# Moving the crossbar transposes, the mask and the casts of a block-sparse attention kernel

## The chip, the cores and the metric

The kernel runs on one core of a Trainium2 chip. The metric is the device time of one execution in microseconds. Before the change it was 378.04 us (median of 2 runs, 377.01 to 379.08). The profile is of one execution; its span, from the first to the last instruction, is about 2 us shorter than the time. A run counts as slow when it is over 1.5% above the fastest of the same kernel; ratios use fast runs alone, while medians are over all runs.

The engines are named as in the profile: PE (TensorE, matmuls), PEld (its weight loads), DVE (VectorE), ACT (ScalarE), POOL (GpSimd) and SP (SyncE, which issues most of the loads). The granted clock is the share of PE's full clock that the profile records. A crossbar transpose is a transpose done by a DMA.

## The reference

```python
# q, k, v: 4 batches x 8 heads x 768 x 64, float32
scores = q @ k.T / sqrt(64)
scores = where(mask, scores, -1e9)   # mask of 24 x 24 blocks of 32: window, edges, 3 random ones a row
attn = softmax(scores); x = attn @ v         # heads laid side by side: 4 x 768 x 512
h = x.T @ U @ V                              # rank 32
u = x + h.T
out = u + relu(u @ w_ch1) @ w_ch2            # 512 -> 2048 -> 512
```

## The kernel before

Heads are worked on in pairs, 16 pairs in all, four to a batch. A pair has six key tiles g and two query halves c, so twelve steps. At each step PE makes the scores of both heads (`psc`), ACT takes the exponential (`est`), and PE multiplies it with v (`pav`). After a pair comes its tail: DVE normalizes (`xs`), POOL casts (`xh`), PE multiplies with U (`pa`) and V (`ph`), DVE adds (`xf`), POOL casts (`uh`), and a crossbar transpose on the SP queue makes `uT`, the input of the MLP. In batches 1 to 3 the MLP of the batch before is cut into small pieces that fill PE between the score steps (`run_fill`). The last MLP runs alone at the end.

Each q and k is loaded, cast to fp16 (`qst`, `kst`) and transposed (`qT`, `kT`).

```python
def load_qk(i, cast):                      # load and cast of pair i, together
    for src, nm in ((q, "q"), (k, "k")):
        ld = ldpool.tile(...)
        nc.sync.dma_start(out=ld, in_=src[...])
        st = stpool.tile(...)
        cast[nm].tensor_copy(out=st..., in_=ld)      # POOL

def turn_dma(sts):                         # crossbar transposes on the SP queue
    for st, nm in zip(sts, "qk"):
        nc.sync.dma_start_transpose(out=tt, in_=st...)

def scores(i, g, c, est, on_pe):
    for h in range(2):                     # two 64-row matmuls
        mm(psc[:, h, 0:HS], kT[rows[h], kc], qT[rows[h], qc], True, not on_pe)
    if on_pe:                              # batch 0: the mask is added by PE
        for h in range(2):
            mm(psc[:, h, 0:HS], kb[rows[h], kc], oh[rows[h], qc], False, True)
    nc.scalar.activation(out=est[:, c], in_=psc[...], func=AF.Exp, scale=0.125)

for i in range(HP):                        # batch 0
    for g in range(T):
        for c in range(2):
            scores(i, g, c, est, True)
            ...                            # value matmuls run two steps behind
        if g == 0: sts[i + 2] = load_qk(i + 2, cast)
        if g == 1: load_v(i + 2)
        if g == 2:
            if i == 1: load_w1()           # 2 MB each, issued from POOL
            if i == 3: load_w2()
        if g == 3:
            qkT[i + 1] = turn_pe(...) if i < 1 else turn_dma(...)

for i in range(HP, NPAIR):                 # batches 1 to 3: the mask is a DVE multiply (mask_mul)
    for g in range(T):
        for c in range(2): scores(i, g, c, est, False)
        ...                                # mask_mul, finish_pair (tail of the pair before), run_fill
        if g == 0: sts[i + 2] = load_qk(i + 2, cast)
        if g == 1: load_v(i + 2)
        if g == 3: qkT[i + 1] = turn_dma(...)
```

The softmax here doesn't subtract the row's maximum and nothing guards it: scores larger than these inputs give would overflow.

## Time and profile before

| | before |
|---|---|
| time | 378.04 us |
| span of the profiled run | 375.2 us |
| PE, ACT, DVE busy | 82%, 47%, 46% |
| mean granted clock of PE | 0.904 |
| pair 4 begins at | 93.7 us |
| last exp begins at | 315.7 us |

"Pair n begins" is the start of every twelfth exponential in the trace, here and below; the "tail" of the tables is what comes after the start of the last one.

Two rows of the page's second part, in which the span is cut into 40 slices of 9.4 us and each digit is a share in tenths:

```profile
PE   1985078850799999795699997987899999999995
PEclk9999559585589999999599999998899999999999
```

PE is idle in the fifth and the tenth slice, and its clock is at half there and just after. The view of waits gives the cause (who waited for whom: us in total, times, longest):

```profile
POOL qst L140 <- DMA qld<-in_q_dram: 33.7, 8, 6.1
...
PE psc L104 <- DMA kT<-kst: 28.4, 3, 14.5
...
PE pa L104 <- POOL xh L331: 15.1, 15, 3.6
...
PE pt L104 <- DMA uT<-uh: 7.8, 3, 4.0
```

POOL stands 33.7 us in q casts whose load has not landed, and PE waits 15.1 us for the `xh` casts that POOL also does. The longest wait of PE, 14.5 us, is for a transposed k. The timeline around it (start, duration, engine, line, operation, in brackets the idle time before it and who ended it):

```profile
30.40 2.15 POOL L262 DMA_DIRECT2D w1t<-in_moe_w_ch_dram  x4
...
31.85 1.78 SPq L181 DMA_TRANSPOSE qT<-qst  x1
...
33.68 10.20 SPq L181 DMA_TRANSPOSE kT<-kst  x1
43.92 0.58 SPq L132 DMA_DIRECT2D qld<-in_q_dram  x1
...
48.17 0.50 PE L104 MATMUL psc<-qT,kT 64*128 64x384 f16 x2 [14.53 <-DMA kT<-kst]
```

The 2 MB of w1 go out at 30.40 us from POOL, the transposes of pair 2 right behind from SP. The second of these keeps the SP queue for 10.20 us and lands, as PE's wait shows, 14.5 us after its issue; a k transpose with no weight load beside it, issued at 61.64 us, landed after 2.6 us. The Trainium skill, "Trainium Kernel Development and Optimization", Key Constraints, says that DMAs of the SP, ACT and POOL queues run on the same 16 DMA engines and interleave. This trace agrees: the transposes were issued from another queue than the weights and were still delayed by them. The same happens with w2 at 75.3 us.

Windows of the same stretch. The columns are the window, its length, then busy us (and instructions) of PE, PEld, DVE, ACT and POOL, the granted clock, the share of the DMA engines, and GB/s:

```profile
30.00:40.00 10.00, 3.64 (x51) 1.72 (x50) 0.00 (x0) 4.24 (x6) 2.55 (x5) 0.91 0.87 147
40.00:50.00 10.00, 1.83 (x14) 0.62 (x14) 0.49 (x2) 0.81 (x1) 0.00 (x0) 0.50 1.17 221
50.00:60.00 10.00, 8.65 (x92) 4.29 (x91) 3.90 (x10) 5.46 (x7) 4.34 (x7) 0.74 0.06 22
```

PE does little for 15 us, and when it starts again it runs at 0.50, then 0.74.

### The profile page before, as it was taken

The numbers are of one execution on the slowest core, as the hardware profiler recorded it, in microseconds if no ns is written. First come the engines' busy times: TensorE is split into PE (matmuls) and PEld (weight loads), VectorE is DVE, ScalarE is ACT, GpSimd is POOL, SyncE is SP. The second block draws the span as 40 slices with busy tenths as digits, with TensorE's granted clock in tenths as the row PEclk, the third lists the DMA queues.
The fourth block names the chain that finished last, engine by engine and source line by source line (L and its number), as shares of the span: only waits on it lengthen the run. The fifth ranks groups of instructions, "written<-read, shape, count | busy, mean of one in ns | idle before, by whom it ended". The sixth has DMA issues, their size and how long they took to land. (4 is left out here: it accounts for less than half of the span.)

```text
span 375.2 us, 6642 instructions
## 1 busy us (share of the span) xinstructions
PE 307.9 (82%) x2759; PEld 155.8 (42%) x2759; DVE 173.8 (46%) x298; ACT 175.8 (47%) x258; POOL 89.9 (24%) x129
## 2 busy tenths in 40 slices
PE   1985078850799999795699997987899999999995
PEld 0342034330345553433255644442456454556442
DVE  3130023330456766455467764563477755444221
ACT  1676037440567765444367754443477663033100
POOL 3734031440232131413131414141121121200000
PEclk9999559585589999999599999998899999999999
DMA  7816944299390044438340906264802011210011
GB/s 241 237 69 104 170 140 89 103 125 163 113 247 2 19 137 112 154 100 217 103 90 2 189 21 204 69 202 54 189 2 65 3 49 58 73 56 2 28 68 72
DMA packets 55657, 38.82 MB, mean 103 GB/s; under 512 B 37548, under 2 KB 52012, under 8 KB 55628
## 3 DMA queue, kind: packets, MB, share of 16 engines
q1 hardware_dynamic: 51760, 33.93, 34.6%
q0 software_dynamic: 3472, 4.24, 7.1%
q8 instruction: 21, 0.34, 0.4%
q10 hardware_dynamic: 396, 0.24, 0.2%
q14 instruction: 8, 0.07, 0.1%
HBM read 27.70 MB, written 6.29 MB: 91 GB/s over the span
## 5 line engine op out<-in xcount | busy, mean ns | idle before, releaser
L301 ACT ACTIVATE est<-psc 128x768 f16<-128x768 f32 x192 | 145.3, 809 | 108.9 <-PE psc L104 108.7
L104 PE MATMUL pt<-uT,w1t 128*128 128x384 f16 x512 | 96.0, 341 | 7.8 <-DMA uT<-uh 7.8
L104 PE MATMUL pch<-w2t,tT 128*128 128x512 f16 x384 | 92.1, 388 | 0.0
L104 PE MATMUL psc<-qT,kT 64*128 64x384 f16 x384 | 58.3, 355 | 29.9 <-DMA kT<-kst 28.4
L308 DVE TENSOR_TENSOR est<-est,m 128x1536 f16<-128x1536 f16 x72 | 71.8, 997 | 0.7 <-ACT est L301 0.6
L104 PEld LDWEIGHTS <-w1t 128*128 128x128 f16 x512 | 49.8, 101 | 44.5 <-issue 18.1
L402 ACT ACTIVATE tT<-pt 128x384 f16<-128x384 f32 x64 | 31.5, 492 | 55.7 <-PE pt L104 55.2
L404 DVE TENSOR_SCALAR tT<-pt 128x384 f16<-128x384 f32 x64 | 35.6, 557 | 46.6 <-PE pt L104 45.7
L104 PEld LDWEIGHTS <-tT 128*128 128x128 f16 x384 | 36.2, 99 | 40.1 <-issue 4.9
L104 PEld LDWEIGHTS <-est 128*128 128x128 f16 x1152 | 41.5, 99 | 26.4 <-issue 25.8
L104 PE MATMUL pav<-vt,est 128*128 128x65 f16 x1152 | 50.5, 197 | 0.0
L373 POOL CAST uh<-xf 128x384 f16<-128x384 f32 x32 | 20.9, 656 | 98.7 <-DVE xf L369 57.9
L104 PEld LDWEIGHTS <-kT 64*128 64x128 f16 x384 | 14.1, 95 | 63.1 <-issue 30.6
L331 POOL CAST xh<-xs 128x384 f16<-128x384 f32 x32 | 20.4, 636 | 71.4 <-DVE xs L324 67.9
L420 DVE TENSOR_TENSOR of<-xf,pch 128x512 f32<-128x512 f32 x24 | 16.5, 687 | 40.6 <-PE pch L104 40.6
L369 DVE TENSOR_TENSOR xf<-xs,ph 128x384 f32<-128x384 f32 x32 | 17.5, 551 | 18.3 <-PE ph L104 18.2
L321 DVE RECIPROCAL rcp<-pav 128x6 f32<-128x6 f32 x32 | 6.2, 195 | 40.8 <-PE pav L104 40.6
L140 POOL CAST qst<-qld 128x768 f16<-128x768 f32 x15 | 12.7, 846 | 51.8 <-DMA qld<-in_q_dram 33.7
L104 PE MATMUL pa<-xh,Ut 128*128 128x128 f16 x96 | 11.0, 239 | 15.4 <-POOL xh L331 15.1
L104 PE MATMUL psc<-oh,kb 64*128 64x384 f16 x96 | 19.7, 385 | 0.5 <-ACT kb L242 0.5
L324 DVE TENSOR_TENSOR xs<-pav,rcp 128x384 f32<-128x384 f32 x32 | 17.8, 557 | 2.1
L359 DVE CAST a<-pa 128x128 f16<-128x128 f32 x16 | 4.6, 288 | 26.4 <-PE pa L104 26.4
(38 smaller groups left out, 94.1 us busy)
## 6 DMA issues: line engine op xcount, KB each, us to landing
qld<-in_q_dram SPq DMA_DIRECT2D x16, 384.0 KB, 3.4
kld<-in_k_dram SPq DMA_DIRECT2D x16, 384.0 KB, 4.3
vld<-in_v_dram SPq DMA_DIRECT2D x16, 384.0 KB, 5.2
out_dram<-of SPq DMA_DIRECT2D x24, 256.0 KB, 2.0
w1t<-in_moe_w_ch_dram POOLq DMA_DIRECT2D x4, 512.0 KB, 11.8
w2t<-in_moe_w_ch_dram POOLq DMA_DIRECT2D x4, 512.0 KB, 11.8
uT<-uh SPq DMA_TRANSPOSE x16, 2.5
qT<-qst SPq DMA_TRANSPOSE x14, 2.5
```

The source lines that it names most:

```text
L104: nc.tensor.matmul(out, lhsT, rhs, start=start, stop=stop, skip_group_check=loose)
L140: keep(cast[nm].tensor_copy(out=st.rearrange("p t h d -> p h t d"), in_=ld))
L301: nc.scalar.activation(out=est[:, c], in_=psc[:, :, 0:HS], func=AF.Exp, scale=0.125)
L308: nc.vector.tensor_tensor(out=est, in0=est, in1=m01[:, g].rearrange("p (c n) -> p c n", c=2)[:, :, None, :] .broadcast_to([P, 2, 2, HS]), ...
L321: keep(nc.vector.reciprocal(out=rcp, in_=pav[:, :, :, D]))
L324: nc.vector.tensor_tensor(out=x3.rearrange("p j (h d) -> p j h d", h=2), in0=pav[:, :, :, 0:D], in1=rcp[:, :, :, None].broadcast_to([P, 3, ...
L331: keep(nc.gpsimd.tensor_copy(out=xh[:, 3 * c : 3 * c + 3, :], in_=x3))
L369: nc.vector.tensor_tensor(out=u3, in0=xs[:, 3 * c : 3 * c + 3, :], in1=ph, op=ALU.add)
L373: keep(nc.gpsimd.tensor_copy(out=uh[:, 3 * c : 3 * c + 3, :], in_=u3))
L402: keep(nc.scalar.activation(out=dst, in_=pt, func=AF.Relu))
L404: keep(nc.vector.tensor_scalar_max(out=dst, in0=pt, scalar1=0.0))
L420: keep(nc.vector.tensor_add(out=of, in0=xfs[b][:, sc, :], in1=pchs[sc]))
```

## The change

Its intent: keep crossbar transposes away from the weight loads by transposing batch 0 on PE; take the mask matmuls off PE; issue the loads of batch 0 further ahead; and cast later than the load is issued, so that POOL does not stand waiting. Cut to its core:

```diff
 # pair 0: the 64 rows of q and of k get 64 mask rows beside them, one 128-row matmul a head
+            if i == 0:
+                mm(psc[:, h, 0:HS], ka[h][:, kc], qa[h][:, qc], True, True)
 # pairs 1 to 3: DVE multiplies instead of mask matmuls on PE
-                scores(i, g, c, est, True)
+                scores(i, g, c, est)
+                if i > 0:
+                    mask_mul(g, est, c)
-    VLAG = 2
+    VLAG = 3                                     # value matmuls three steps behind
-                later.extend(pair_tail(i, xs, xh))
+                later.extend([(0, lambda: None)] * 2 + pair_tail(i, xs, xh))
 # pairs 1 to 4: transposed by PE, one tensor at a time
-                qkT[i + 1] = turn_pe(sts.pop(i + 1)) if i < 1 else turn_dma(sts.pop(i + 1))
+                if i < 3 and u in (6, 8): ... turn_pe(i + 1, nm); nc.vector.tensor_copy(...)
+                if i == 3 and u in (8, 10): ... the same
 # batches 1 to 3
+            if g == 0:
+                turn_dma(i + 1, "q"); turn_dma(i + 1, "k"); issue(i + 2)
+            if g == 2:
+                cast(i + 2, "q")
+            if g == 4:
+                cast(i + 2, "k"); cast(i + 2, "v")
-            if i == HP and g == 2:
+            if i == HP and g == 4:
                 fill.extend(mlp_steps(0))
-            if g == 0 and i + 2 < NPAIR:
-                sts[i + 2] = load_qk(i + 2, cast)
-            if g == 1 and i + 2 < NPAIR:
-                load_v(i + 2)
-            if g == 3 and i + 1 < NPAIR:
-                qkT[i + 1] = turn_dma(sts.pop(i + 1))
# (cut: places of the loads in batch 0, the building of the 0/1 mask moved into pair 0, the last value matmuls of batch 0 spread over pair 4, buffer counts)
```

More of the change, by code (lines that the diff above doesn't have):

```diff
@@ L66 @@
     pos = (cols % P) * T + cols // P
-    oh_np = np.zeros((2, D, S), dtype=np.float16)
-    oh_np[:, :NB] = (pos[None, :] // BLK == ii[:, None])[None]
-    oh_np = oh_np.reshape(P, S)
+    oh_np = np.zeros((D, S), dtype=np.float16)
+    oh_np[:NB] = pos[None, :] // BLK == ii[:, None]
     eye16_np = np.eye(P, dtype=np.float16)
@@ L80 @@
     stpool = ctx.enter_context(tc.tile_pool(name="stpool", bufs=2))
-    qkpool = ctx.enter_context(tc.tile_pool(name="qkpool", bufs=3))
+    qkpool = ctx.enter_context(tc.tile_pool(name="qkpool", bufs=2))
     epool = ctx.enter_context(tc.tile_pool(name="epool", bufs=10))
@@ L109 @@
     id16 = consts.tile([P, P], FP16)
-    oh = consts.tile([P, S], FP16)
-    kb = consts.tile([P, S], FP16)
+    qa = [consts.tile([P, S], FP16, name=f"qa{h}") for h in range(2)]
+    ka = [consts.tile([P, S], FP16, name=f"ka{h}") for h in range(2)]
     m01 = consts.tile([P, T, S], FP16)
@@ L123, with issue @@
     rows = [slice(0, D), slice(D, P)]
-    def load_qk(i, cast):
+    mrows = [slice(D, P), slice(0, D)]
+    lds, sts, qkT = {}, {}, {}
+    NPAIR = B * HP
+    def issue(i, names="qkv"):
+        if i >= NPAIR:
+            return
         b, hp = divmod(i, HP)
-        sts = []
-        for src, nm in ((q, "q"), (k, "k")):
+        for nm in names:
             ld = ldpool.tile([P, 2, T, D], FP32, tag="ld" + nm, name=nm + "ld")
+            src = {"q": q, "k": k, "v": v}[nm]
             keep(
@@ L138, in load_qk, with cast @@
             )
-            st = stpool.tile([P, T, 2, D], FP16, tag="st" + nm, name=nm + "st")
-            keep(cast[nm].tensor_copy(out=st.rearrange("p t h d -> p h t d"), in_=ld))
-            sts.append(st)
-        return sts
-    def load_v(i):
-        b, hp = divmod(i, HP)
-        ld = ldpool.tile([P, 2, T, D], FP32, tag="ldv", name="vld")
+            lds[i, nm] = ld
+    def cast(i, nm, eng=None):
+        if i >= NPAIR:
+            return
+        b, hp = divmod(i, HP)
+        ld = lds.pop((i, nm))
+        if nm == "v":
+            keep(
+                nc.gpsimd.tensor_copy(
+                    out=vts[b % 2][:, 2 * hp : 2 * hp + 2, :, 0:D], in_=ld
+                )
+            )
+            return
+        st = stpool.tile([P, T, 2, D], FP16, tag="st" + nm, name=nm + "st")
@@ L147, in load_v, with turn_pe @@
         keep(
-            nc.sync.dma_start(
-                out=ld,
-                in_=v[b, 2 * hp : 2 * hp + 2].rearrange("h (p t) d -> p h t d", t=T),
-            )
-        )
+            (eng or nc.gpsimd).tensor_copy(
+                out=st.rearrange("p t h d -> p h t d"), in_=ld
+            )
+        )
+        sts[i, nm] = st
+    def turn_pe(i, nm):
+        st = sts.pop((i, nm))
+        pt = pst_tile([P, T, P], FP16, "pturn")
+        for t in range(T):
+            keep(
+                nc.tensor.transpose(
+                    out=pt[:, t, :],
+                    in_=st[:, t].rearrange("p h d -> p (h d)"),
+                    identity=id16,
+                )
+            )
+        return pt
@@ L153, in load_v, with new_turn, turn_dma @@
+    def new_turn(i, nm):
+        qkT[i, nm] = qkpool.tile([P, T, P], FP16, tag=nm + "T", name=nm + "T")
+        return qkT[i, nm]
+    def turn_dma(i, nm):
+        if i >= NPAIR:
+            return
+        st = sts.pop((i, nm))
         keep(
-            nc.gpsimd.tensor_copy(
-                out=vts[b % 2][:, 2 * hp : 2 * hp + 2, :, 0:D], in_=ld
-            )
-        )
-    def turn_pe(sts):
-        ts = []
-        for st, nm in zip(sts, "qk"):
-            pt = pst_tile([P, T, P], FP16, "pturn")
-            for t in range(T):
-                keep(
-                    nc.tensor.transpose(
-                        out=pt[:, t, :],
-                        in_=st[:, t].rearrange("p h d -> p (h d)"),
-                        identity=id16,
-                    )
-                )
-            tt = qkpool.tile([P, T, P], FP16, tag=nm + "T", name=nm + "T")
-            keep(nc.vector.tensor_copy(out=tt, in_=pt))
-            ts.append(tt)
-        return ts
@@ L176, in turn_dma @@
-    def turn_dma(sts):
-        ts = []
-        for st, nm in zip(sts, "qk"):
-            tt = qkpool.tile([P, T, P], FP16, tag=nm + "T", name=nm + "T")
-            keep(
-                nc.sync.dma_start_transpose(
-                    out=tt, in_=st.rearrange("p t h d -> p (t h d)")
-                )
-            )
-            ts.append(tt)
-        return ts
+            nc.sync.dma_start_transpose(
+                out=new_turn(i, nm), in_=st.rearrange("p t h d -> p (t h d)")
+            )
+        )
@@ L192 @@
     nc.scalar.dma_start(out=small[0:NB, :], in_=small_dr.ap())
+    nc.scalar.dma_start(out=id16, in_=eye16_dr.ap())
     nc.scalar.dma_start(out=dup[0:NB], in_=dup_dr.ap())
-    nc.scalar.dma_start(out=id16, in_=eye16_dr.ap())
-    nc.scalar.dma_start(out=oh, in_=oh_dr.ap())
-    sts = {}
-    qkT = {}
-    sts[0] = load_qk(0, {"q": nc.vector, "k": nc.gpsimd})
+    for h in (1, 0):
+        nc.scalar.dma_start(out=qa[h][mrows[h], :], in_=oh_dr.ap())
+    issue(0)
+    issue(1)
     for vt in vts:
@@ L218 @@
         prev = a01[0:NB]
+        if r == 0:
+            cast(0, "q", nc.vector)
     keep(
@@ L224 @@
     )
+    cast(0, "k")
+    pq = turn_pe(0, "q")
     pb = pst_tile([P, 2 * D], FP32, "pb")
@@ L231 @@
     )
-    qkT[0] = turn_pe(sts.pop(0))
+    pk = turn_pe(0, "k")
     pm = pscp.tile([P, 2, 512], FP32, tag="psc", name="pm")
@@ L237 @@
             bias[0:NB].rearrange("k a z -> k (a z)"),
-            oh[0:NB, c * HS : (c + 1) * HS],
+            qa[1][0:NB, c * HS : (c + 1) * HS],
             True, True,
         )
-    keep(
-        nc.scalar.copy(
-            out=kb.rearrange("z (c n) -> z c n", c=2), in_=pm[:, :, 0:HS]
-        )
-    )
-    def load_mix():
-        nc.gpsimd.dma_start(
-            out=Ut[:, :, 0:R], in_=moe_U.rearrange("(p t) r -> p t r", t=T)
-        )
-        vld = ldpool.tile([P, S], FP32, tag="ldv", name="mvld")
-        keep(nc.sync.dma_start(out=vld[0:R, :], in_=moe_V))
+    flat = "p t n -> p (t n)"
+    keep(nc.vector.tensor_copy(out=qa[0][rows[0], :], in_=pq[rows[0]].rearrange(flat)))
+    keep(nc.scalar.copy(out=qa[1][rows[1], :], in_=pq[rows[1]].rearrange(flat)))
+    keep(nc.vector.tensor_copy(out=ka[0][rows[0], :], in_=pk[rows[0]].rearrange(flat)))
+    keep(nc.scalar.copy(out=ka[1][rows[1], :], in_=pk[rows[1]].rearrange(flat)))
+    for h, eng in ((0, nc.vector.tensor_copy), (1, nc.scalar.copy)):
         keep(
-            nc.gpsimd.tensor_copy(
-                out=Vt[0:R, :, :], in_=vld[0:R, :].rearrange("r (p t) -> r t p", t=T)
-            )
-        )
+            eng(
+                out=ka[h][mrows[h], :].rearrange("z (c n) -> z c n", c=2),
+                in_=pm[mrows[h], :, 0:HS],
+            )
+        )
+    cast(0, "v")
+    nc.gpsimd.dma_start(
+        out=Ut[:, :, 0:R], in_=moe_U.rearrange("(p t) r -> p t r", t=T)
+    )
+    mvld = opool.tile([P, S], FP32, tag="mv", name="mvld", bufs=1)
+    keep(nc.sync.dma_start(out=mvld[0:R, :], in_=moe_V))
     def load_w1():
@@ L276, in load_w2, with mask_tile, scores @@
             )
-    def mask_tile(g):
-        for c in range(2):
-            pmk = pst_tile([P, HS], FP32, "pmk")
-            mm(pmk, kb[0:D, g * P : (g + 1) * P], oh[0:D, c * HS : (c + 1) * HS],
-               True, True)
-            keep(
-                nc.vector.tensor_scalar(
-                    out=m01[:, g, c * HS : (c + 1) * HS], in0=pmk,
-                    scalar1=-1.0, scalar2=None, op0=ALU.is_ge,
-                )
-            )
-    def scores(i, g, c, est, on_pe):
-        qT, kT = (t.rearrange("p t n -> p (t n)") for t in qkT[i])
+    def mask_tile(g, c):
+        pmk = pst_tile([P, HS], FP32, "pmk")
+        mm(pmk, ka[1][0:D, g * P : (g + 1) * P], qa[1][0:D, c * HS : (c + 1) * HS],
+           True, True)
+        keep(
+            nc.vector.tensor_scalar(
+                out=m01[:, g, c * HS : (c + 1) * HS], in0=pmk,
+                scalar1=-1.0, scalar2=None, op0=ALU.is_ge,
+            )
+        )
+    def scores(i, g, c, est):
         psc = pscp.tile([P, 2, 512], FP32, tag="psc", name="psc")
@@ L295, in scores @@
         for h in range(2):
-            mm(psc[:, h, 0:HS], kT[rows[h], kc], qT[rows[h], qc], True, not on_pe)
-        if on_pe:
-            for h in range(2):
-                mm(psc[:, h, 0:HS], kb[rows[h], kc], oh[rows[h], qc], False, True)
+            if i == 0:
+                mm(psc[:, h, 0:HS], ka[h][:, kc], qa[h][:, qc], True, True)
+            else:
+                qT, kT = (qkT[i, nm].rearrange(flat) for nm in "qk")
+                mm(psc[:, h, 0:HS], kT[rows[h], kc], qT[rows[h], qc], True, True)
         keep(
@@ L304, in scores, with mask_mul @@
         )
-    def mask_mul(g, est):
-        keep(
-            nc.vector.tensor_tensor(
-                out=est, in0=est,
-                in1=m01[:, g].rearrange("p (c n) -> p c n", c=2)[:, :, None, :]
-                .broadcast_to([P, 2, 2, HS]),
-                op=ALU.mult,
-            )
-        )
+    def mask_mul(g, est, c=None):
+        if c is None:
+            o = est
+            m = m01[:, g].rearrange("p (c n) -> p c n", c=2)[:, :, None, :]
+            m = m.broadcast_to([P, 2, 2, HS])
+        else:
+            o = est[:, c]
+            m = m01[:, g, None, c * HS : (c + 1) * HS].broadcast_to([P, 2, HS])
+        keep(nc.vector.tensor_tensor(out=o, in0=o, in1=m, op=ALU.mult))
     xfs, uTs = {}, {}
@@ L452, in pair_tail @@
         ]
-    NPAIR = B * HP
-    cast = {"q": nc.gpsimd, "k": nc.gpsimd}
-    load_v(0)
-    sts[1] = load_qk(1, cast)
-    load_mix()
-    load_v(1)
     later = deque()
@@ L494 @@
                     flush_value()
-                if later and c == 1:
+                if later:
                     later.popleft()[1]()
-            if g == 0 and i + 2 < NPAIR:
-                sts[i + 2] = load_qk(i + 2, cast)
-            if g == 1:
-                load_v(i + 2)
-            if g == 2:
-                if i == 1:
-                    load_w1()
-                if i == 3:
-                    load_w2()
-            if g == 3:
-                qkT[i + 1] = turn_pe(sts.pop(i + 1)) if i < 1 else turn_dma(sts.pop(i + 1))
@@ L508 @@
-            if i >= 2 and g % 2 == 1:
-                mask_tile((i - 2) * 3 + g // 2)
-    while pend:
-        flush_value()
+                u = 2 * g + c
+                if i == 0 and u >= 2:
+                    mask_tile((u - 2) // 2, u % 2)
+                if i == 0:
+                    if u == 0:
+                        cast(1, "q")
+                        cast(1, "k")
+                    if u == 1:
+                        keep(
+                            nc.gpsimd.tensor_copy(
+                                out=Vt[0:R, :, :],
+                                in_=mvld[0:R, :].rearrange("r (p t) -> r t p", t=T),
+                            )
+                        )
+                        cast(1, "v")
+                        issue(2)
+                        issue(3)
+                    if u == 6:
+                        cast(2, "q")
+                        cast(2, "k")
+                        cast(2, "v")
@@ new lines @@
+                if i == 1:
+                    if u == 0:
+                        mask_tile(5, 0)
+                        mask_tile(5, 1)
+                        load_w1()
+                    if u == 4:
+                        cast(3, "q")
+                        cast(3, "k")
+                        cast(3, "v")
+                        issue(4)
+                    if u == 8:
+                        issue(5)
+                if i == 2:
+                    if u == 8:
+                        cast(4, "q")
+                        cast(4, "k")
+                        cast(4, "v")
+                    if u == 10:
+                        load_w2()
@@ new lines @@
+                if i == 3:
+                    if u == 8:
+                        cast(5, "q")
+                        cast(5, "k")
+                        cast(5, "v")
+                if i < 3 and u in (6, 8):
+                    nm = "qk"[u // 2 - 3]
+                    pt = turn_pe(i + 1, nm)
+                    keep(nc.vector.tensor_copy(out=new_turn(i + 1, nm), in_=pt))
+                if i == 3 and u == 2:
+                    pass
+                if i == 3 and u in (8, 10):
+                    nm = "qk"[u // 2 - 4]
+                    pt = turn_pe(i + 1, nm)
+                    keep(nc.vector.tensor_copy(out=new_turn(i + 1, nm), in_=pt))
@@ L552 @@
             for c in range(2):
-                scores(i, g, c, est, False)
+                scores(i, g, c, est)
+                if i == HP and (pend or later):
+                    if pend:
+                        flush_value()
+                    elif later:
+                        later.popleft()[1]()
             if g > 0:
@@ L557 @@
                 mask_mul(T - 1, prior[1][T - 1])
-            spent = 0.0
-            if i == HP and later:
-                while later:
-                    cost, fn = later.popleft()
-                    fn()
-                    spent += cost
+            if g == 0:
+                turn_dma(i + 1, "q")
+                turn_dma(i + 1, "k")
+                issue(i + 2)
+            if g == 2:
+                cast(i + 2, "q")
+            if g == 4:
+                cast(i + 2, "k")
+                cast(i + 2, "v")
+            spent = 0.0
             if prior is not None:
                 spent += finish_pair(prior, g)
-            if i == HP and g == 2:
+            if i == HP and g == 4:
                 fill.extend(mlp_steps(0))
@@ L570 @@
             run_fill(FILL - spent)
-            if g == 0 and i + 2 < NPAIR:
-                sts[i + 2] = load_qk(i + 2, cast)
-            if g == 1 and i + 2 < NPAIR:
-                load_v(i + 2)
-            if g == 3 and i + 1 < NPAIR:
-                qkT[i + 1] = turn_dma(sts.pop(i + 1))
         prior = (i, ests, xs, xh)
```

## The prediction

> **What bounds the kernel now.** The page gives a 375.2 us span, PE 82% busy, ACT 47%, DVE 46%. The table of windows shows two holes in PE in the first batch: 33.4 to 48.2 us and 80.5 to 93.1 us. The view of waits names them: PE waits 28.4 us in three waits for the crossbar transpose of k, the longest 14.5 and 12.55 us. The timeline says why: the 2 MB w1 load is issued at 30.4 us and the 2 MB w2 load at 75.3 us, just ahead of the transposes, which sit behind them (the k transpose holds the SP queue 10.2 and 4.3 us; usually 1.2 us). After each hole the windows show a granted clock of 0.50 to 0.77 for 10 to 30 us: pairs 2 and 3 take about 16 us each, pair 1 about 13.5 us. The Trainium skill, "TensorE: Matmul & The Clock Gate", Part 1, says an idle window of about 3.4 us halves the clock; this trace agrees (0.50 after both holes).
> After 93 us the kernel is PE-bound: an unhindered pair takes 16.3 us. There PE still idles about 20 us, 12.0 us of it waiting for POOL's xh cast; POOL was blocked in q casts that wait for their load (33.7 us). Clock drops follow (near 155, 178, 253, 263 us), some 8 us more. The last 59 us are MLP matmuls alone.
>
> **What the change does.**
> - Batch 0 and the first pair of batch 1 use no crossbar transposes: 6 TensorE transposes (0.3 us) and one DVE copy (0.56 us) for each of q and k. Both holes should go: 27 us, plus about 6 us of slow clock after each.
> - Pairs 1 to 3 lose the mask matmuls and get DVE multiplies of 128x768, about 0.52 us each (half of the 997 ns of 128x1536). DVE then has per pair 12x0.52 + norm 1.5 + a 0.3 + xf 1.1 + copies 1.1 = 10.3 us, 11.4 us in pair 1 with two mask tiles; ACT has 12x0.735 = 8.8 us. So they become DVE-bound: 11.5 to 12 us each.
> - Pair 0 keeps the mask in the contraction: about as before, 10.5 us. First exp near 12.4 us (12.3 before).
> - Steady state: transposes and loads at step 0, casts at steps 2 and 4, so POOL rarely waits. The first MLP starts two steps later, so its end moves nearer to the next one's start (the lack of filler at 173 to 188 us).
>
> **Sum.** Pair 4 starts near 12.4+10.5+36 = 59 us (93 before). Pair 4 about 15 us, 11 pairs of 16.3 us = 179 us: 253 us. Tail 59 us: 312 us. Stalls and slow clock that remain: 9 us. The time exceeds the span by 2 to 3 us: **324 us**, range 313 to 340. Chances: faster by over 2% 0.96, within 2% 0.03, slower 0.01.
>
> **What shows it.** Right: no PE wait over 3 us for kT or qT before 60 us; mask multiplies of 128x768 x36 at 0.50 to 0.55 us; the first pt matmul between 63 and 72 us (98 before); DVE over 85% busy between 25 and 55 us; PE's wait for xh after that below 5 us; mean clock above 0.95; the last 59 us unchanged. Wrong: pairs 1 to 3 over 13 us each, or new waits of POOL on loads, or of PE on uT.
>
> **What would make it wrong.** DVE-bound pairs leave PE half idle, and the clock may be halved there; PE waits in order for DVE, so latencies may add to DVE's sum. In 57 us some 11 MB must be loaded, about 200 GB/s of the 240 to 300 GB/s seen: loads could be late. The slow phases after 150 us may have causes that I missed, and remain.

## The result

The kernel after takes 340.95 us (median of 2 runs, 339.85 to 342.04). The ratio to before is 0.9019, with a 95% interval of 0.8855 to 0.9183. Ratios in this document are the mean time of one kernel's fast runs over that of the other's fast runs of the same rounds, so not quite the ratio of the medians quoted. Two later groups of runs, on other chips, gave 340.80 and 341.92 us for the same kernel. The direction was right and the size was not: 324 was predicted, and 340 was the upper end of the range.

| | before | after | predicted |
|---|---|---|---|
| span | 375.2 | 340.0 | 321 |
| mean granted clock | 0.904 | 0.929 | over 0.95 |
| pair 0 | 11.1 | 12.7 | 10.5 |
| pairs 1 to 3 together | 70.3 | 41.5 | 36 |
| pair 4 begins at | 93.7 | 66.8 | 59 |
| pair 4 | 20.3 | 18.9 | 15 |
| pairs 5 to 15, to the last exp | 201.7 | 195.3 | 179, and 9 for stalls |
| tail | 59.4 | 59.0 | 59 |

The same two rows of the page after (slices of 8.5 us):

```profile
PE   2696977888999999958999999959999999999995
PEclk9999678755999999996999999987999999999999
```

The two holes are gone. But the clock is low from the fifth to the tenth slice, and dips of PE remain at slices 18 and 27. The waits after:

```profile
POOL qst L160 <- DMA qld<-in_q_dram: 7.8, 8, 1.9
...
PE pt L103 <- DMA uT<-uh: 10.1, 3, 4.0
...
PE pa L103 <- POOL xh L340: 8.8, 11, 1.3
...
PE psc L103 <- DVE kT L555: 1.6, 1, 1.6
```

No wait of PE for a crossbar transpose of k is left, and POOL's wait for q fell from 33.7 to 7.8 us. PE's wait for `uT` is not smaller but larger, 10.1 us in three waits. The windows that answer to those of before:

```profile
30.00:40.00 10.00, 8.37 (x87) 4.97 (x86) 7.10 (x14) 5.81 (x8) 5.00 (x6) 0.66 0.41 88
40.00:50.00 10.00, 7.56 (x88) 4.97 (x86) 7.83 (x17) 6.48 (x9) 4.27 (x6) 0.80 0.22 78
50.00:60.00 10.00, 8.09 (x95) 4.66 (x93) 7.74 (x16) 7.23 (x11) 6.02 (x8) 0.84 0.85 136
```

These are pairs 1 to 3. No engine is full: DVE, predicted to bound them, is 71 to 78% busy, and the clock is 0.66 to 0.84. This is how the start of pair 2 looks in the timeline (between these lines stand others):

```profile
42.55 0.77 POOL L340 CAST xh<-xs 128x384 f16<-128x384 f32 x1 [7.40 <-DVE xs L333]
42.87 0.19 DVE L330 RECIPROCAL rcp<-pav 128x6 f32<-128x6 f32 x1
43.09 0.56 DVE L333 TENSOR_TENSOR xs<-pav,rcp 128x384 f32<-128x384 f32 x1
...
43.57 1.32 DVE L323 TENSOR_TENSOR est<-est,m 128x768 f16<-128x768 f16 x2
43.72 0.77 POOL L340 CAST xh<-xs 128x384 f16<-128x384 f32 x1 [0.39 <-DVE xs L333]
44.53 0.33 PE L103 MATMUL pa<-xh,Ut 128*128 128x128 f16 x3 [0.83 <-POOL xh L340]
44.80 0.34 PE L103 MATMUL psc<-qT,kT 64*128 64x384 f16 x2
...
45.17 1.60 ACT L310 ACTIVATE est<-psc 128x768 f16<-128x768 f32 x2 [1.86 <-PE psc L103]
```

DVE normalizes between mask multiplies, POOL casts, PE waits 0.83 us for the cast with `pa`, and the scores of the next step stand behind `pa`; so ACT idles 1.86 us. The Trainium skill, "TensorE: Matmul & The Clock Gate", Part 2, says that matmuls stay in program order and only weight loads are pulled ahead. This trace agrees: the scores at 44.80 us start only after `pa`, although their inputs were there long before.

At pair 8 the other leftover shows, first in the timeline, then in the windows:

```profile
151.93 1.22 SPq L387 DMA_TRANSPOSE uT<-uh  x1
...
154.46 4.30 PE L103 MATMUL pt<-uT,w1t 128*128 128x384 f16 x13 [3.54 <-DMA uT<-uh]
```

```profile
150.00:155.00 5.00, 1.46 (x10) 0.73 (x9) 1.33 (x2) 1.19 (x3) 1.62 (x2) 0.68 0.35 86
155.00:160.00 5.00, 5.00 (x22) 2.19 (x21) 1.77 (x3) 1.89 (x4) 0.00 (x0) 0.64 0.80 235
```

The MLP of the batch before starts in the very step that issues its last `uT`. PE waits 3.54 us for it and then runs at about 0.64 for 5 us. (The clock record has only full and half; it fell to half at 151.8 us, inside the wait, and rose at 158.6.)

### The profile page after: what moved, and what is told of

Same layout as the page of the kernel before. It is cut to its first block, busy times and chain, and to the rows that moved or that the text cites. A ratio compares the mean times of both kernels' runs of the same rounds, so it can differ in the third digit from the quotient of the medians.

```text
span 340.0 us, 6559 instructions
## 1 busy us (share of the span) xinstructions
PE 302.9 (89%) x2699; PEld 158.6 (47%) x2699; DVE 197.1 (58%) x341; ACT 178.0 (52%) x260; POOL 101.1 (30%) x129
## 3 DMA queue, kind: packets, MB, share of 16 engines
q1 hardware_dynamic: 46960, 32.74, 33.7%
## 5 line engine op out<-in xcount | busy, mean ns | idle before, releaser
L103 PE MATMUL pt<-uT,w1t 128*128 128x384 f16 x512 | 97.1, 344 | 10.1 <-DMA uT<-uh 10.1
L323 DVE TENSOR_TENSOR est<-est,m 128x1536 f16<-128x1536 f16 (+1 forms) x108 | 93.7, 871 | 9.5 <-ACT est L310 9.2
L103 PE MATMUL pch<-w2t,tT 128*128 128x512 f16 x384 | 89.1, 379 | 0.0
L340 POOL CAST xh<-xs 128x384 f16<-128x384 f32 x32 | 22.8, 712 | 117.4 <-DVE xs L333 111.4
L103 PE MATMUL psc<-qT,kT 64*128 64x384 f16 x360 | 53.8, 353 | 3.5 <-DVE kT L555 1.6
L103 PEld LDWEIGHTS <-tT 128*128 128x128 f16 x384 | 35.5, 98 | 38.2 <-issue 1.6
L103 PEld LDWEIGHTS <-est 128*128 128x128 f16 x1152 | 43.2, 100 | 18.9 <-issue 13.9
L378 DVE TENSOR_TENSOR xf<-xs,ph 128x384 f32<-128x384 f32 x32 | 17.5, 549 | 2.9 <-PE ph L103 2.7
L160 POOL CAST kst<-kld 128x768 f16<-128x768 f32 x16 | 17.5, 1092 | 2.3 <-DMA kld<-in_k_dram 2.3
L103 PE MATMUL pa<-xh,Ut 128*128 128x128 f16 x96 | 10.0, 225 | 8.9 <-POOL xh L340 8.8
L153 POOL CAST vt<-vld 128x768 f16<-128x768 f32 x16 | 16.9, 1056 | 2.5 <-DMA vld<-in_v_dram 2.4
L160 POOL CAST qst<-qld 128x768 f16<-128x768 f32 x15 | 15.2, 1011 | 7.8 <-DMA qld<-in_q_dram 7.8
```

The costliest lines, as they stand in the source:

```text
L103: nc.tensor.matmul(out, lhsT, rhs, start=start, stop=stop, skip_group_check=loose)
L153: nc.gpsimd.tensor_copy(out=vts[b % 2][:, 2 * hp : 2 * hp + 2, :, 0:D], in_=ld)
L160: (eng or nc.gpsimd).tensor_copy(out=st.rearrange("p t h d -> p h t d"), in_=ld)
L323: keep(nc.vector.tensor_tensor(out=o, in0=o, in1=m, op=ALU.mult))
L340: keep(nc.gpsimd.tensor_copy(out=xh[:, 3 * c : 3 * c + 3, :], in_=x3))
L378: nc.vector.tensor_tensor(out=u3, in0=xs[:, 3 * c : 3 * c + 3, :], in1=ph, op=ALU.add)
```

## The experiments

The theory after seeing the result: the gain has two sources, the crossbar transposes in batch 0 and the late casts in batches 1 to 3; the missing 17 us have two causes, pairs 1 to 3 and the waits for `uT`. Rivals for pairs 1 to 3: DVE's sum of work, the half clock, or the waits in order. Except where it is said, the edits are to the kernel after, and all runs gave the right result. Runs 1 to 4, 5 to 8, 9 to 12, 13 to 16 and 17 to 18 shared a chip each, with the kernel before run beside them (medians 375.27, 374.33, 375.75, 373.58 and 373.89 us). Runs of different groups are compared by their ratios to before.

### 1. The transposes alone, in the kernel before

```diff
-                qkT[i + 1] = turn_pe(sts.pop(i + 1)) if i < 1 else turn_dma(sts.pop(i + 1))
+                qkT[i + 1] = turn_pe(sts.pop(i + 1)) if i < HP else turn_dma(sts.pop(i + 1))
```

> The kernel before, with one part of the change alone: q and k of pairs 1 to 4 are transposed by TensorE, nothing else moves. If the gain of 37 us is the two holes behind the weight loads (28.4 us of waits for the transposes of k, and the half clock after them), this alone gives 25 to 38 us: 340 to 353 us. If the gain came from the mask form or from the order of loads and casts, it stays above 365 us.

Measured: 354.94 us, ratio 0.9462 (0.9401 to 0.9524). This is 20 us of gain, less than expected. Pairs 1 to 3 take 43.9 us in place of 70.3, against 41.5 in the kernel after. So within batch 0 the PE transposes give nearly everything that the change gave there; the rest of it (mask form, places of the loads, slack) adds little in sum.

### 2. Crossbar transposes given back to batch 0

```diff
+                if i in (1, 2, 3) and u == 7:
+                    turn_dma(i + 1, "q"); turn_dma(i + 1, "k")
-                if i < 3 and u in (6, 8):
+                if i < 1 and u in (6, 8):
-                if i == 3 and u in (8, 10):
+                if False:
```

> The kernel after, with q and k of pairs 2 to 4 given back to the crossbar, in step 3 of the pair before, as the kernel before had them; weight loads stay where the change put them. If it was the place of the weight loads just ahead of the transposes that cost the time, the first hole stays away (w1 is now issued at 17 us) and a hole of 5 to 15 us comes at pair 3 or 4, beside the w2 load issued at 51 us: 345 to 360 us. If moving the loads had been enough: within 3 us of 341. If crossbar transposes are slow there by themselves: over 365.

Measured: 350.23 us, ratio 0.9318 (0.9263 to 0.9372), so some 5 to 11 us slower than after (ratios of 0.9019 to 0.9180 in its groups). PE waits 14.6 us for `kT` in three waits, at the start of pairs 2, 3 and 4. The issue of each transpose, and who waited for it:

```profile
36.82 1.29 SPq L188 DMA_TRANSPOSE kT<-kst  x1
39.43 0.50 PE L103 MATMUL psc<-qT,kT 64*128 64x384 f16 x2 [3.52 <-DMA kT<-kst]
...
52.77 1.24 SPq L188 DMA_TRANSPOSE kT<-kst  x1
53.01 2.99 POOL L280 DMA_DIRECT2D w2t<-in_moe_w_ch_dram  x4
58.72 0.10 PEld L103 LDWEIGHTS <-kT 64*128 64x128 f16 x2 [7.07 <-DMA kT<-kst]
...
72.14 1.28 SPq L188 DMA_TRANSPOSE kT<-kst  x1
74.76 0.50 PE L103 MATMUL psc<-qT,kT 64*128 64x384 f16 x2 [4.16 <-DMA kT<-kst]
```

Only the second landed late: it was issued just before the weights and landed about 6 us later, where the other two took 2.6 us. These two were issued late instead. In the SP queue they stand behind the `uT` transpose of the pair before (issued at 34.14, 50.13 and 69.54 us), which waits for that pair's tail. So crossbar transposes cost PE time here in two ways: at least 7.7 us of the waits come from the order of the SP queue, and a transpose in the company of a bulk load lands late. In the kernel before it was mostly the second: the k transposes of the two holes landed 14.5 and 14.2 us after their issue.

### 3. The old order of casts and transposes in batches 1 to 3

```diff
-            if g == 0: turn_dma(i + 1, "q"); turn_dma(i + 1, "k"); issue(i + 2)
-            if g == 2: cast(i + 2, "q")
-            if g == 4: cast(i + 2, "k"); cast(i + 2, "v")
             run_fill(FILL - spent)
+            if g == 0: issue(i + 2, "qk"); cast(i + 2, "q"); cast(i + 2, "k")
+            if g == 1: issue(i + 2, "v"); cast(i + 2, "v")
+            if g == 3: turn_dma(i + 1, "q"); turn_dma(i + 1, "k")
```

> The kernel after, with the order of before in batches 1 to 3: casts right behind the issue of their loads, transposes at step 3. Theory: the new order saves PE waits for xh (12.0 us before, a good part of 8.8 after) and a few clock drops: 4 to 12 us slower than after. Rival: the holes were everything and the order of casts is worth nothing: within 2 us.

Measured: 359.70 us, ratio 0.9594 (0.9532 to 0.9656). The kernel after had ratios of 0.9019, 0.9165 and 0.9180 in its groups, so the old order of casts and transposes together costs 16 to 22 us: more than the theory's 4 to 12. With the 20 us of run 1 this makes up the gain of 37 us. Run 1 and this run shared a chip, and between them lies the rest of the change: with it the kernel is 4.8 us slower (ratios 0.9594 and 0.9462, intervals apart). So the rest, the mask form among it, was no gain but a loss.

### 14. Only the casts in their old place

```diff
-            if g == 2: cast(i + 2, "q")
-            if g == 4: cast(i + 2, "k"); cast(i + 2, "v")
             run_fill(FILL - spent)
+            if g == 0: issue(i + 2, "qk"); cast(i + 2, "q"); cast(i + 2, "k")
+            if g == 1: issue(i + 2, "v"); cast(i + 2, "v")
```

> The kernel after, with only the casts (and the load of v) of batches 1 to 3 in their old place, behind the issue of their loads; transposes stay at step 0. If POOL standing in a cast that waits for its load is the cause: 12 us or more slower than after, as when both were undone (19 us), with PE's wait for xh over 10 us past 67 us. If the place of the transposes was the cause: within 4 us of after.

Measured: 374.74 us, ratio 1.0043 (0.9980 to 1.0106): the whole gain is gone. The kernel after on the same chip took 341.92 us. The waits:

```profile
POOL qst L160 <- DMA qld<-in_q_dram: 55.2, 8, 13.3
```

```profile
PE pa L103 <- POOL xh L340: 28.6, 21, 3.4
```

POOL stands 55.2 us in q casts that wait for their load, and PE waits 28.6 us for the `xh` casts behind them. It is worse than run 3 (35.0 and 18.7 us): here the two transposes stand ahead of the loads in the SP queue (in one pair at 104.65 and 105.94 us, the q load at 107.27) while the cast is at once behind. So with early casts the transposes at step 0 do harm. Whether they gain anything with late casts was not run.

### 4. The mask of pairs 1 to 3 on PE again

```diff
-                mm(psc[:, h, 0:HS], kT[rows[h], kc], qT[rows[h], qc], True, True)
+                mm(psc[:, h, 0:HS], kT[rows[h], kc], qT[rows[h], qc], True, i >= HP)
+        if 0 < i < HP:
+            for h in range(2):
+                mm(psc[:, h, 0:HS], ka[1 - h][rows[h], kc], qa[1 - h][rows[h], qc], False, True)
-                if i > 0:
-                    mask_mul(g, est, c)
```

> The kernel after, with the mask of pairs 1 to 3 added by TensorE again (two 64-row matmuls a step) in place of the 36 DVE multiplies. If DVE's sum bounds these pairs (the prediction), they shrink from about 13.5 us to ACT's 9 to 11 us: 333 to 336 us. If they are bound by PE waiting in order for POOL, DVE and PSUM at the pair's start and by the half clock: 338 to 343 us, with DVE below 55% busy there.

Measured: 335.05 us, ratio 0.8911 (0.8866 to 0.8957). Pairs 1 to 3 take 10.5, 10.0 and 10.0 us in place of 14.4, 13.5 and 13.6, 11.0 us less in sum, and pair 4 begins at 54.4 us, 12.4 us earlier. The DVE multiplies are a net loss. But the kernel gains only some 4 to 10 us by the ratios; part of the rest is told at run 17.

### 7. and 8. Half clock, or DVE's work?

Run 7 keeps the multiplies and gives PE the mask matmuls as needless work, to keep its clock up. Run 8 has the mask on PE, as run 4, and lets DVE multiply a tile that nobody waits for.

```diff
 # run 7
+                if i < HP:
+                    mm(psc[:, h, 0:HS], ka[1 - h][rows[h], kc], qa[1 - h][rows[h], qc], True, True)
                 mm(psc[:, h, 0:HS], kT[rows[h], kc], qT[rows[h], qc], True, True)
 # run 8: run 4, and
-                    mask_mul(g, est, c)
+                    nc.vector.tensor_tensor(out=scr, in0=scr, in1=m01[...], op=ALU.mult)
```

> The kernel after, with two needless 64-row matmuls of the mask put ahead of the score matmuls of pairs 1 to 3 (overwritten by these), so PE has as many matmuls as with the mask on PE, and DVE still has its 36 multiplies. If the half clock in these pairs (0.79 on average) is what makes them 13.5 us instead of 11.5: the clock goes to 0.95 or more, they take 11 to 12 us, and the time falls by 4 to 7 us. If DVE's queue and the waits in order are the cause, pairs stay over 13 us.

> The mask of pairs 1 to 3 on PE as in the fourth run, but DVE still executes the 36 multiplies of 128x768, on a tile that nothing waits for. If DVE's sum of work bounds these pairs: they take 12 us or more. If it is the multiply in the path from exp to the value matmul: 10 to 11 us, as in the fourth run.

Measured: run 7 341.04 us, ratio 0.9155 (0.9058 to 0.9253), equal to after on the same chip (run 5: 340.80 us, 0.9165). Pairs 1 to 3 take 13.3, 12.5 and 14.5 us. Run 8: 336.57 us, ratio 0.9043 (0.8960 to 0.9126), with pairs of 11.8, 10.9 and 11.8 us. The windows over pairs 1 to 3, first of after, then of run 7, then of run 8:

```profile
25.00:66.00 41.00, 32.34 (x361) 19.50 (x360) 32.33 (x65) 27.77 (x37) 20.53 (x25) 0.79 0.67 128
```

```profile
26.00:66.00 40.00, 32.81 (x433) 17.22 (x432) 32.83 (x66) 27.78 (x37) 20.41 (x25) 0.96 0.67 130
```

```profile
27.00:61.00 34.00, 30.70 (x430) 16.34 (x428) 32.92 (x66) 27.46 (x37) 21.20 (x25) 1.00 0.66 129
```

In run 7 the clock is 0.96 and the three pairs take 40.2 us in place of 41.5: raising the clock this way brings back only 1.3 us. But pairs 1 and 2, at full clock throughout (0.76 and 0.75 in after), were each about 1 us shorter, and that with needless work in PE. So some of the excess can be the clock's; run 7 does not separate the two. In run 8 DVE does the same 32.9 us of work in 34 us, 97% busy: this is what a DVE bound looks like, 11.5 us a pair, as predicted. In after the same DVE work needs 41 us. The difference, 2.3 us a pair, is not DVE's work.

### 9. and 13. Slack at the ends of the chain

```diff
 # run 9
-                later.extend([(0, lambda: None)] * 2 + pair_tail(i, xs, xh))
+                later.extend([(0, lambda: None)] * 4 + pair_tail(i, xs, xh))
 # run 13: run 9, and
-    VLAG = 3
+    VLAG = 5
-            if i == HP and g == 4:
+            if i == HP and g == 5:
```

> The kernel after, with four empty places in place of two ahead of each pair's tail in batch 0, so the pa matmul comes two steps later and its xh is long cast. If PE's waits in order at the start of a pair (5.3 us of waits for xh between 27 and 66 us, and DVE multiplies queued ahead of the normalization) make up what the pairs took beyond DVE's sum (13.8 us against the 11.5 of the run with idle multiplies): pairs 1 to 3 fall to 11.5 to 12.5 us, the time by 3 to 6 us. If the cause is the multiply between exp and the value matmul itself: no change.

> The kernel after, with slack at both ends of the chain in batch 0: value matmuls five steps behind the scores in place of three, and four empty places ahead of the tail in place of two (the first MLP then starts at step 5 in place of 4). If PE, waiting in order for DVE and POOL, makes pairs 1 to 3 longer than DVE's sum: they fall from 13.8 to 11.5 to 12.3 us, and the time by 4 to 6 us. If they stay over 13 us, the order of waits is not the cause.

Measured: run 9 339.75 us, ratio 0.9086 (0.8980 to 0.9193), no different from after. Run 13: pairs 1 to 3 take 11.4, 11.1 and 13.0 us, 35.5 in place of 41.5, and DVE is 95% busy:

```profile
26.00:61.00 35.00, 27.85 (x359) 17.89 (x356) 33.42 (x65) 26.40 (x37) 20.84 (x25) 0.96 0.64 124
```

So it was the waits in order, with whatever the half clock that came with them adds: with slack for the value matmuls and for `pa`, pairs 1 and 2 come back to DVE's sum, and pair 3 does in part. PE's wait for `xh` in this stretch falls from 5.3 to 0.9 us. At full clock in both, pairs 1 and 2 together take 22.5 us here and 25.8 in run 7. Which of the two slacks did it was not separated. The total does not follow: 343.81 us (one of the four runs slow), ratio 0.9200 (0.9136 to 0.9264), the same as after on that chip (0.9180). The expected 4 to 6 us did not come. Pair 4 begins 5 us earlier, but the start of the MLPs is later by a step and PE's wait for `uT` grows to 13.0 us, and later pairs are longer. This part is not settled by a run.

### 11. Pair 0 as before

```diff
-                mm(psc[:, h, 0:HS], ka[h][:, kc], qa[h][:, qc], True, True)
+                mm(psc[:, h, 0:HS], ka[h][rows[h], kc], qa[h][rows[h], qc], True, False)
+                # and, once a step: two 64-row mask matmuls, as in run 4
```

> The kernel after, with pair 0 scored as before: two 64-row matmuls and two 64-row mask matmuls a step in place of two 128-row ones. Two 64-row ones take the time of one[...], so both forms cost PE about the same: pair 0 within 0.5 us, the time within 1% of after. If the 128-row form was a gain, pair 0 grows by over 1 us.

Measured: 341.20 us, ratio 0.9159 (0.9084 to 0.9234), equal to after; pair 0 takes 12.1 us, where three profiles of after show 12.5 to 15.0. The 128-row form is worth nothing that these runs resolve. (What the expectation says of two 64-row matmuls is seen in the kernel before: at 30.67 us two of them start 3 ns apart and take 0.33 us each, as one 128-row matmul does at 19.15 us in after.)

### 5., 6. and 16. The MLP started later, and after itself

```diff
-            if i == HP and g == 4:
+            if i == HP + 1 and g == 0:
                 fill.extend(mlp_steps(0))
-            if hp == 0 and b > 1 and g == 5:
+            if hp == 1 and b > 1 and g == 0:
                 fill.extend(mlp_steps(b - 1))
```

> The kernel after, unchanged, so that the other runs of this group have it on the same chip. 338 to 343 us, 0.90 of before.

> The kernel after, with each interleaved MLP started at step 0 of the second pair of the next batch in place of step 5 (the first MLP: step 4) of the first, so that its last uT is long there. Theory: three waits of PE for uT (10.1 us) and the half clock after each are the largest part of what stayed after 67 us; they go, and the time falls by 8 to 18 us, to 323 to 333 us, with pairs 8 and 12 near 17 us (23 now). Rival: PE then only runs out of filler in the same places, pairs 8 and 12 stay over 21 us and the time is within 4 us of after.

> The kernel after, unchanged, on the same chip as the three: 338 to 343 us.

Measured: run 6 330.29 us, ratio 0.8876 (0.8772 to 0.8980), against 340.80 us and 0.9165 (0.9043 to 0.9286) for after on the same chip (run 5), and 341.92 us and 0.9180 (0.9109 to 0.9252) on another (run 16). PE's wait for `uT` falls to 1.2 us; pairs 8 and 12 take 17.5 and 17.0 us in place of 23.1 and 22.9. The rival, that PE would only run out of filler in the same places, falls: 10.5 us were there to be had. That is about what the waits themselves were (10.1 us); how much of it is the slow clock after them, and how much was given back where the later MLP work went (the tail grew from 59.0 to 61.6 us), this run does not tell.

### 10., 12. and 15. Together

Run 10 is run 4 with run 6; run 12 adds the four empty places of run 9; run 15 is run 10 with a third correction:

```diff
-            if g == 2:
+            if g == (4 if i == HP else 2):
                 cast(i + 2, "q")
-            if g == 4:
+            if g == (5 if i == HP else 4):
                 cast(i + 2, "k"); cast(i + 2, "v")
```

> Both gains together: the mask of pairs 1 to 3 on PE, and each interleaved MLP begun one pair later. Fourth run minus 5 us and sixth run minus 10 us against after; if they add: 323 to 328 us, faster than both kernels.

> The tenth kernel with the four empty places as well. With the mask on PE, waits for xh in batch 0 are 0.5 us only, so this should be worth nothing: within 2 us of the tenth.

> The tenth kernel, with the casts of the first pair of batch 1 moved to steps 4 and 5. There uh of pair 3 stood behind a q cast that waited for its load, so uT was 3.2 us late at the first MLP, and 5 us at half clock followed. If that is right the wait is below 1 us, pair 5 falls from 24.3 to 18 to 20 us, and the time by 3 to 6 us, to 319 to 322 us.

Measured: run 10 324.48 us, ratio 0.8690 (0.8623 to 0.8757): the two gains add. Run 12 323.38 us, ratio 0.8672 (0.8606 to 0.8737), the same. Run 15 323.98 us, ratio 0.8673 (0.8621 to 0.8726): PE's wait for `uT` fell from 4.4 to 2.3 us and pair 5 from 24.5 to 22.4 us, less than expected, and the time did not move measurably.

### 17. and 18. What was given back

In run 4 pair 10 took 20.8 us, where it is 17.4 in after, though both run the same program there. The timeline of run 4 shows why:

```profile
173.81 0.83 POOL L160 CAST qst<-qld 128x768 f16<-128x768 f32 x1 [2.20 <-DMA qld<-in_q_dram]
174.59 1.23 POOL L343 CAST xh<-xs 128x384 f16<-128x384 f32 x1
...
175.87 0.44 PE L103 MATMUL pa<-xh,Ut 128*128 128x128 f16 x3 [1.83 <-POOL xh L343]
176.10 3.72 PE L103 MATMUL pt<-uT,w1t 128*128 128x384 f16 x12
```

The q cast at step 2 came 2.20 us too early, `xh` stood behind it, PE idled 1.83 us, and then, at half clock, twelve matmuls took 3.72 us where they take 2.11 at full clock. Run 17 moves the cast behind `xh`, in the kernel of run 15; run 18 is run 15 again.

```diff
-            if g == (4 if i == HP else 2):
+            if g == (4 if i == HP else 3):
                 cast(i + 2, "q")
```

> The fifteenth kernel with the q cast at step 3 in place of 2, behind the xh cast. If q casts that wait for their load are what makes single pairs 1 to 3 us longer: POOL's waits for qld cost PE nothing more, PE's wait for xh falls from 6.5 us past 67 us to below 3, pairs 7 to 15 are none over 18 us, and the time falls by 2 to 5 us, to 318 to 322 us. Rival: these waits are overlapped, within 1 us.

> The fifteenth kernel unchanged, on the same chip: 322 to 325 us.

Measured: run 17 319.55 us, ratio 0.8579 (0.8490 to 0.8668); run 18 321.97 us, ratio 0.8659 (0.8587 to 0.8730). PE's wait for `xh` past 67 us is 2.8 us in place of 6.0, and pairs 7 to 15 are none over 17.7 us. The medians differ by 2.4 us and the four times of each do not overlap (318.08 to 320.63 against 321.53 to 323.67), but the intervals of the ratios do. This is the fastest kernel, 16 to 23 us below after by the ratios.

## Why the prediction was wrong

Point by point:

- **Two holes behind the weight loads.** Right. They went, and run 1 shows that the PE transposes alone bring 20 us, less than the 27 us plus clock of the prediction.
- **Late casts keep POOL from waiting.** Right in mechanism, and larger than it looked: 16 to 22 us are lost when casts and transposes both go back (run 3), 33 us when the casts go back alone (run 14).
- **"So they become DVE-bound: 11.5 to 12 us each".** This is the first step that failed: pairs 1 to 3 took 13.8 us each on average. DVE's sum was right (run 8: 11.5 us, DVE 97% busy). But the prediction took an engine's sum for the time of a stage in which PE, DVE and POOL wait for each other in order. The excess is 2.3 us a pair, 7 us in all, and 6 of it go when the chain gets slack (run 13). The prediction named both dangers, waits that add to DVE's sum and a halved clock, but gave them no time. The half clock was there (0.79). Raising it with needless work brought back 1.3 of the 7 us (run 7); what it adds to the waits by itself stays open. Within the sum the multiply was mis-sized too, 622 ns in place of 520, as this group of the list by shape shows:

```profile
L323 DVE TENSOR_TENSOR est<-est,m 128x768 f16<-128x768 f16 x36 | 22.1, 622 | 8.4 <-ACT est L310 8.1
```

- **"Stalls and slow clock that remain: 9 us".** This is the second step that failed. Pairs 5 to 15 took 195.3 us, 16 over the 179 of unhindered pairs, and pair 4, for which no stall was allowed, took 3.9 us over its 15. The prediction put the slow phase of 173 to 188 us down to a lack of filler and expected it to shrink. Run 6 shows what it was: the interleaved MLP starts in the step that issues its last `uT`, PE waits 2.5 to 4 us three times and runs slowly after. The waits were in the trace of before (7.8 us), but the prediction's account of before does not mention them; starting the MLP later was worth 10.5 us. In pair 4 the clock was low before the wait for `uT`: it fell to half at 66.4 us, just as PE came out of the 1.6 us wait for DVE's copy of `kT`, and stayed there until 83.5. In run 6 it fell in the same place. What that copy of the PE transpose cost was not tried.
- **Pair 0.** 10.5 us predicted, 12.7 measured (12.5 to 15.0 over three profiles). The 128-row matmul is not the cause (run 11). The traces show where the scatter comes from: PE starts slow. Two score matmuls take 0.82 us at first and 0.50 later, and the switch comes at another moment in each run. First after, then run 5:

```profile
17.62 0.82 PE L103 MATMUL psc<-qa,ka 128*128 128x384 f16 x2
18.97 0.50 PE L103 MATMUL psc<-qa,ka 128*128 128x384 f16 x2
```

```profile
23.27 0.82 PE L103 MATMUL psc<-qa,ka 128*128 128x384 f16 x2
25.06 0.49 PE L103 MATMUL psc<-qa,ka 128*128 128x384 f16 x2
```

The profile's clock record begins only here, so the tables count the stretch before it as full clock. It begins 5.7, 6.1 and 11.5 us after the first exp in runs 16, after and 5, with pair 0 at 12.5, 12.7 and 15.0 us. In before it is 5.3 us, with pair 0 at 11.1, so by this comparison about 1 us remains that the start does not explain. That stays open; the mask tiles that now stand in pair 0 were not tried elsewhere.
- **Tail of 59 us.** Right, 59.0.

The terms add up: 0.2 us for the first exp, 2.2 for pair 0, 5.5 for pairs 1 to 3, 3.9 for pair 4 and 7.3 for pairs 5 to 15 beyond their 9 us make 19.1, which is 340.0 less the predicted span of 320.9.

Of the signs listed, these held: no wait for transposed k, PE's wait for `xh` below 5 us past 67 us (3.4), the tail. These failed: the multiplies' mean, the first `pt` matmul (74.2 us, predicted 63 to 72), DVE over 85% busy (77% between 25 and 55 us), the clock over 0.95 (0.929). Of the signs of error that it named, pairs over 13 us came, and waits of PE for `uT`, though these were not new.

Open: why part of the time won in batch 0 is lost again later. For run 4 one such place is shown (the q cast of pair 10), and moving that cast brought 2.4 us. For run 13 none was shown.

## What to carry to other kernels

An engine's sum of work bounds a stage only if the chain between the engines has slack; where in-order engines pass small pieces around, first look for who waits at the hand-overs, and give those places a step or two of distance. That alone need not pay in the total: here it brought the pairs back but not the time (run 13), while moving the mask back to PE brought both (run 4). A cast or any other instruction that waits for a load, put early in an in-order queue, holds up everything behind it: place it where its input is surely there, and check again after each other change. A short wait of PE can cost more than its length: in run 4 a wait of 1.83 us was followed by a stretch at half clock in which twelve matmuls took 1.6 us longer. And a transpose or load in an in-order queue can be late because of what stands ahead of it there, not because it is slow: compare issue and landing before moving it to another engine.

## What the Trainium skill lacked or had wrong

- "TensorE: Matmul & The Clock Gate", Part 1, ties the half clock to an idle window of about 3.4 us, and says that frequent micro-idles between groups of matmuls also make the clock oscillate; it gives no size for these. In run 4 the clock fell after PE had idled 1.83 us (twelve matmuls in 3.72 us against 2.11), and in pairs 1 to 3 of after the mean clock was 0.79 although no wait of PE there was longer than 1.2 us and PE was 79% busy. In the 3.4 us before each of the three falls in these pairs (at 32.3, 46.0 and 59.6 us) PE was busy 52 to 54% of the time.
- "SBUF — State Buffer", SBUF: two separate sides, says that a DVE op with two SBUF inputs and a GpSimd op that reads SBUF lock each other out for a whole instruction. The traces fit in direction: the `xh` cast in batch 0 takes 0.51 us before and 0.77 us beside the mask multiplies, and of the 36 multiplies 28 take 0.55 us and eight, all with a POOL cast beside them, 0.70 to 1.17. The page gives no size for a mixed stream. Eleven of the 28 short ones had a POOL cast beside them too. That the lock is the reason was not tried.
- "DMA: Bandwidth & Descriptors", DMA Transpose (X-bar), gives no time to landing, alone or beside a bulk load. Here a 128x768 fp16 transpose out of SBUF landed about 2.5 us after issue (median of `qT` and `uT`), and two k transposes behind a 2 MB weight load from another queue landed 14.5 and 14.2 us after theirs.
